# Attention loads in half as many transfers: q and k of four heads together, heads paired differently, and the division of two quads moved behind the next norms

## The chip, the cores and the metric

The kernel runs on one core of one Trainium2 chip. The metric is the device time of one execution in microseconds; lower is better. Times of "before" are the median of three runs, and one more execution was recorded by the hardware profiler. TensorE is called PE, VectorE DVE, ScalarE ACT, GpSimd POOL and SyncE SP.

## The reference

Attention with normalised queries and keys, followed by a feed-forward block on the heads joined together:

```python
batch, n_heads, seq, head_dim = (8, 12, 448, 64)
def rmsnorm(x, g):
    rms = np.sqrt(np.mean(x * x, axis=-1, keepdims=True) + 1e-06)
    return x / rms * g
q_n, k_n = (rmsnorm(q, g_q), rmsnorm(k, g_k))
scores = scale * np.matmul(q_n, k_n.transpose(0, 1, 3, 2))
scores = scores - np.max(scores, axis=-1, keepdims=True)
attn = np.exp(scores)
attn = attn / (np.sum(attn, axis=-1, keepdims=True) + 1e-09)
attn_out = np.matmul(attn, v)
x = np.ascontiguousarray(attn_out.transpose(0, 2, 1, 3)).reshape(B * S, H * D)
# x: 3584 x 768; h = x @ w_in (768 x 1024); SoLU; layer norm; @ w_out (1024 x 768)
```

q, k and v arrive in float32, the weights in float64.

## The kernel before

The work on the chip is `fast_path`, which has three stages that follow one another on PE: attention for 24 *quads* of four heads, the first feed-forward product and the second one (both by a scheme of seven products for eight). The change lies in the first stage, which ends at about 331 us.

A quad m consists of the pairs a = 2m and b = 2m + 1 of two heads each. For a pair n the steps are, with their lines in the profile:

- `load(n)` (L627): q and k of the two heads, each head in four quarters, go to 32 partitions at a time. That is eight transfers of 56 KB (L634) into a tile `qk`, of which five exist. `load_v(m)` (L639) brings v of a quad: one transfer for the first 384 keys (`v`, L647), two for the last 64 keys (`vl`, L651).
- `squares(n)` (ACT, L656), `row_sums(n)` (DVE, L664, tile `part`), and for a whole quad `fold_sums(m)` (POOL, L674 and L675, tile `ss`).
- `rsqrt_seed` (ACT, L694 and L695, tile `ny`), `rsqrt_step` (DVE, L701 to L704, tiles `nx` and `ny`), `normalise(n)` (POOL, L713, tile `qkn`), `qk_transpose(n)` (DVE, L723, tile `qkT`), `gain(n)` (ACT, L727).
- `scores(n, kc)` (PE, L812, tile `s`), three times for a pair, and `scores_last(m)` (PE, L825) for the last keys of both pairs. Behind each stands an exponential (ACT, L802, tile `E`).
- `add(n)` (DVE, L839, tile `es`), a part of the row sums.
- `values_last(m)` (PE, L854) and `values(n)` (PE, L865), E times v into the PSUM tile `o`. Two such tiles exist, one for each pair of a quad.
- `sums(m)` (PE, L884, tile `sm`), `inverse(m)` (DVE, L895 and L896, then copies on POOL, L903, tile `rc`), `divide(m)` (DVE, twice L910 and L911, reads both `o` and writes `xo`), `store_x(m)` (SP, L916) into the DRAM tensor `xd`, from which the second stage loads.

The first quad's q and k are loaded otherwise (`load_rows`, L732).

The order is written out by hand: within `tc.manual_schedule()` each engine carries out its instructions in the order in which the functions are called. In the body for quad m the norms of quad m + 1 are finished (`norms_next`), the squares and sums of quad m + 2 are taken, and q and k of quad m + 3 are loaded. `unit(f)` calls a piece of PE work; `later(1, f)` has f called after the next unit. So `later(1, lambda m=m: divide(m))` at the end of quad m puts the division behind scores(a, 0) of quad m + 1. For m > 4 `norms_next` comes before that, for m = 1, 2 and 3 after it (`early` is false).

All loads and stores of this stage are issued by SP, one after another, and an issue that has to wait holds up those behind it. Each transfer's landing is told by one of eight semaphores in turn, and an issue waits for the transfer that used its semaphore before.

Of the kernel before, what the change touches and what calls it, by code (L numbers as in the profile page):

```python
# [9 lines left out]
FP32 = mybir.dt.float32  # L10
# [3 lines left out]
AF = mybir.ActivationFunctionType  # L14
# [352 lines left out]
def fast_path(  # L367
# [38 lines left out]
    R = S // 4  # L406
# [12 lines left out]
    loads = first.enter_context(tc.tile_pool(name="loads", bufs=2))  # L419
# [8 lines left out]
    xd = [dram.tile([DM, S], FP32, name=f"xd{b}") for b in range(B)]  # L428
# [189 lines left out]
    st = {}  # L618
    quads = {}
    norms = {}  # L620

    def load(n):  # L627
        b, hp = divmod(n, NP)
        h0 = 2 * hp
        d = st[n] = {}  # L630
        d["qk"] = loads.tile([P, 2, NB, 32], FP32, tag="qk", name="qk", bufs=5)
        for s, src in enumerate((q, k)):
            for g in range(4):
                nc.sync.dma_start(  # L634
                    d["qk"][g * 32 : g * 32 + 32, s],
                    src[b, h0 + g // 2].rearrange("(b t) (x d) -> x t b d", t=32, x=2)[g % 2],
                )

    def load_v(m, queue=nc.sync):  # L639


        d = quads[m] = {}
        b, hp = divmod(2 * m, NP)
        src = v[b, 2 * hp : 2 * hp + 4]
        d["v"] = loads.tile([P, 4, NJ, D], FP32, tag="v", name="v", bufs=2)
        d["vl"] = loads.tile([P, 2, D], FP32, tag="vl", name="vl", bufs=2)
        queue.dma_start(  # L647
            d["v"].rearrange("p h j d -> p h (j d)"), src[:, 0 : NJ * P].rearrange("h (p j) d -> p h (j d)", j=NJ)
        )
        for i in range(2):  # L650
            nc.sync.dma_start(d["vl"][i * D : (i + 1) * D], src[2 * i : 2 * i + 2, NJ * P : S].rearrange("h p d -> p h d"))  # L651

    def squares(n):
        d = st[n]
        d["sq"] = work.tile([P, 2 * NB, 32], FP32, tag="sq", name="sq", bufs=2)
        nc.scalar.activation(d["sq"], d["qk"].rearrange("p s b d -> p (s b) d"), AF.Square)  # L656

# [48 lines left out]
    def normalise(n, e=nc.gpsimd):  # L706
        d = st[n]
        if ("one", n) in norms:
            y = norms["one", n]["y"]
        else:  # L710
            y = norms[n // 2]["y"][:, n % 2 * 2 * NB : (n % 2 + 1) * 2 * NB]
        d["qkn"] = work.tile([P, 2 * NB, 32], FP32, tag="qkn", name="qkn", bufs=2)
        e.tensor_tensor(  # L713
            d["qkn"],
            d["qk"].rearrange("p s b d -> p (s b) d"),
            y.rearrange("p b -> p b ()").to_broadcast([P, 2 * NB, 32]),
            OP.mult,
        )

# [12 lines left out]
    def load_rows(n, queues):  # L732
        b, hp = divmod(n, NP)
        d = st[n] = {}
        d["qk"] = xs.tile([P, 2, 4, P], FP32, tag="x", name="x")[0:R]
        for s, src in enumerate((q, k)):
            for h in range(2):
                queues[2 * s + h].dma_start(
                    d["qk"][:, s, :, h * D : (h + 1) * D], src[b, 2 * hp + h].rearrange("(j p) d -> p j d", p=R)
                )  # L740

    def square_rows(n, s, engine):
# [61 lines left out]
    def scores(n, kc):  # L804
        d = st[n]
        s = ps_t.tile([P, 2, 512], FP32, tag="t", name="s")

        for c in range(0, P, D):
            for h in range(2):
                hh = slice(h * D, (h + 1) * D)  # L810
                keys = slice(NJ * c + kc, NJ * (c + D - 1) + kc + 1, NJ)
                nc.tensor.matmul(  # L812
                    s[c : c + D, h, 0:S], d["qkT"][hh, 1, keys], d["qkT"][hh, 0, :],
                    start=True, stop=True,
                )
        exponentials(d, kc, s)
# [42 lines left out]
    def values(n):  # L859


        d = st[n]
        for kc in range(NJ):
            for h in range(2):
                nc.tensor.matmul(  # L865
                    d["o"][h * D : (h + 1) * D, :], quads[n // 2]["v"][:, n % 2 * 2 + h, kc], d["E", kc][:, h],
                    start=False, stop=(kc == NJ - 1),
                )

# [43 lines left out]

    def store_x(m):
        b, hp = divmod(2 * m, NP)
        nc.sync.dma_start(  # L916
            xd[b].rearrange("(c p) t -> p c t", p=P)[:, hp : hp + 2], quads.pop(m)["xo"]
        )

# [427 lines left out]
    setup()  # L1347
    load_gains()
    load_rows(1, (nc.sync, nc.sync, nc.scalar, nc.scalar))
    load(2)  # L1350
    load(3)
    load_v(0)
    load(4)
    load_norm_gain()
    load(5)
    with tc.manual_schedule():
        warm_up()
        square_rows(0, 0, nc.vector)
# [17 lines left out]
        for m in range(NQ):  # L1376
            a, b = 2 * m, 2 * m + 1
# [6 lines left out]
            next1 = m + 1 < NQ  # L1384
            next2 = m + 2 < NQ
            next3 = m + 3 < NQ
            if m == 0:
                unit(lambda: scores(a, 0))
                normalise_rows(1, 0)
                normalise_rows(1, 1)  # L1390
                unit(lambda: scores(a, 1))
                unit(lambda: scores(a, 2))
                for s in range(2):
                    transpose_rows(1, s)
                    take_rows(1, s)
# [12 lines left out]
                unit(lambda: scores(b, 1))  # L1408
                unit(lambda: scores(b, 2))
                rsqrt_seed(norms["one", 3])  # L1410
                rsqrt_step(norms["one", 3])
                normalise(3)
                qk_transpose(2)
                gain(2)
                add(b)
                load_v(1)
                load(6)
                load(7)
                unit(outputs)
# [12 lines left out]
            early = 3 < m and next1  # L1432
            def norms_next():
                rsqrt_seed(norms[m + 1])
                rsqrt_step(norms[m + 1])
                normalise(a + 2)
                normalise(b + 2)
# [4 lines left out]
                combine_in(x)  # L1442
            if next1:
                load_v(m + 1)
            unit(lambda: scores(a, 0))
            store_x(m - 1)
            if early:
                qk_transpose(a + 2)
                if next3:
                    load(a + 6)  # L1450
            if m == 3:
                norms_next()
            unit(lambda: scores(a, 1))
            if m == 2:
                norms_next()
            unit(lambda: scores(a, 2))
            if m == 3:
                qk_transpose(a + 2)
                load(a + 6)
            unit(lambda: scores_last(m))  # L1460
            if m == 3:
                norm_gain()
# [2 lines left out]
            unit(lambda: scores(b, 0))  # L1465
            if m == 1:
                norms_next()
                load(a + 6)
                load(b + 6)
            if m == 2:  # L1470
                qk_transpose(a + 2)
                load(a + 6)
            unit(lambda: scores(b, 1))
            if early or 1 < m < 4:
                qk_transpose(b + 2)
                if next3:
# [239 lines left out]
```

## Time and profile before

| | us |
|---|---|
| median of 3 runs | 823.92 (823.67 to 824.59) |
| the profiled execution | 824.07 |
| its span, from the first to the last instruction | 821.8 |
| PE busy in it | 800.8 |
| first `s` matmul of quad 1 / last matmul of the attention | 26.09 / about 331.6 |

The span is 2.3 us shorter than the execution's time. DMA packets of the execution: 272546, of which 190540 are under 512 bytes; q and k arrive in runs of 128 bytes.

```profile
qk<-in_q_dram SPq DMA_DIRECT2D x184, 56.0 KB, 2.6
qk<-in_k_dram SPq DMA_DIRECT2D x184, 56.0 KB, 2.4
v<-in_v_dram SPq DMA_DIRECT2D x24, 384.0 KB, 4.4
vl<-in_v_dram SPq DMA_DIRECT2D x48, 32.0 KB, 3.5
xd<-xo SPq DMA_DIRECT2D x24, 448.0 KB, 3.6
```

These lines of the list of transfers give the tile and its source, the queue, the number of transfers, the size of one, and the median time in us from issue to landing. A busy PE is read with care: its ends are modelled, and a gap shows only where an instruction really waited. In the timelines below a row joins neighbouring instructions of one line; its columns are start, length, engine, line, operation, tiles, shapes and count, and in brackets the idle time before it with what ended it.

### The profile page before, as it was taken

How to read it: one execution, taken by the hardware profiler on the slowest of the kernel's cores; microseconds unless marked ns; L12 is line 12 of the kernel's file. 1: busy time of each engine (PE TensorE's matmuls, PEld its weight loads, DVE VectorE, ACT ScalarE, POOL GpSimd, SP SyncE). 2: the span in 40 equal slices, each digit the busy share in tenths (PEclk: the TensorE clock that was granted, in tenths of full speed). 3: DMA queues.
4: the chain of work that ended last, by engine and by line, in shares of the span. 5: the costliest groups of instructions: out<-in, count | busy, mean ns of one | idle time of the engine just before them, and what ended most of it. 6: DMA issues, size and time to landing. Idle time of an engine off the chain costs nothing.

```text
span 821.8 us, 14997 instructions
## 1 busy us (share of the span) xinstructions
PE 800.8 (97%) x5030; PEld 469.7 (57%) x5030; DVE 616.3 (75%) x1217; ACT 475.3 (58%) x785; POOL 469.9 (57%) x635
## 2 busy tenths in 40 slices
PE   8989999999999999999999999999989999999996
PEld 4333444443344443444444444444689999999996
DVE  6867788887878888377878766677786866866945
ACT  6667778776867777366666644444514464464420
POOL 1334546555555647333356467777487777877861
PEclk9999999999999999999999999999999999999999
DMA  6678777877777664235665335453548466376312
GB/s 130 131 146 197 141 187 151 205 148 176 159 175 175 128 158 119 87 103 127 185 166 153 94 95 136 131 143 73 160 122 270 126 211 231 127 243 203 125 59 82
DMA packets 272546, 122.74 MB, mean 149 GB/s; under 512 B 190540, under 2 KB 257612, under 8 KB 272460
## 3 DMA queue, kind: packets, MB, share of 16 engines
q1 hardware_dynamic: 257276, 111.79, 52.9%
q10 hardware_dynamic: 15184, 9.90, 4.5%
q8 instruction: 42, 0.69, 0.4%
q14 instruction: 44, 0.36, 0.2%
HBM read 84.94 MB, written 36.70 MB: 148 GB/s over the span
## 4 chain that ended last, share of the span: by engine, by line
PE 71%; SPq 6%; DMA 5%; DVE 5%; issue 2%; POOL 2%; ACT 1%; DVEq 0%; POOLq 0%; ACTq 0%
PE A L1196 14%; PE A L982 11%; PE B L1196 7%; PE o L865 7%; PE s L812 7%; PE B L982 7%; SPq L634 5%; PE C L982 4%; PE D L982 4%; PE C L1196 4%; PE sm L884 3%; DMA v<-in_v_dram 2%; PE s L825 1%; PE o L854 1%; DMA qk<-in_k_dram 1%
## 5 line engine op out<-in xcount | busy, mean ns | idle before, releaser
L802 ACT ACTIVATE E<-s 128x896 f32<-128x896 f32 x168 | 139.0, 935 | 15.5 <-PE s L812 15.2
L812 PE MATMUL s<-qkT 64*64 64x448 f32 x1152 | 121.1, 547 | 1.5 <-ACT E L802 0.9
L865 PE MATMUL o<-E,v 128*64 128x448 f32 x576 | 113.5, 543 | 0.0
L674 POOL COPY ss<-part 32x56 f32<-32x56 f32 x88 | 42.1, 478 | 97.5 <-DVE part L664 94.8
L713 POOL TENSOR_TENSOR qkn<-qk,ny 128x896 f32<-128x896 f32 x46 | 77.1, 1697 | 27.5 <-DVE ny L704 12.0
L1071 POOL TENSOR_TENSOR he<-he,mhalf 128x1 f32<-128x1 f32 x28 | 27.6, 986 | 105.7 <-DVE he L1070 105.3
L1196 PE MATMUL B<-w_out,sums 128*128 128x192 f32 x392 | 80.4, 328 | 3.3 <-DVE P L1258 2.1
L812 PEld LDWEIGHTS s<-qkT 64*64 64x64 f32 x1152 | 47.7, 163 | 60.7 <-ACT E L802 30.9
L1196 PE MATMUL A<-w_out,sums 128*128 128x192 f32 x392 | 80.6, 329 | 1.0 <-POOL sums L1177 0.7
L865 PEld LDWEIGHTS o<-E,v 128*64 128x64 f32 x576 | 39.2, 137 | 72.7 <-issue 65.2
L982 PE MATMUL B<-w_in,xsum 128*128 128x512 f32 x168 | 76.7, 593 | 0.7 <-POOL he L1071 0.7
L982 PE MATMUL A<-w_in,xg 128*128 128x512 f32 x168 | 74.7, 593 | 0.1
L1196 PEld LDWEIGHTS B<-w_out,sums 128*128 128x128 f32 x392 | 66.9, 191 | 3.9 <-DVE P L1258 2.4
L1053 ACT ACTIVATE u<-h,hmax 128x1024 f32<-128x1024 f32 x28 | 32.2, 1148 | 63.3 <-DVE hmax L1047 63.2
L1196 PEld LDWEIGHTS A<-w_out,sums 128*128 128x128 f32 x392 | 66.8, 191 | 1.7 <-POOL sums L1177 1.6
L982 PEld LDWEIGHTS B<-w_in,xsum 128*128 128x128 f32 x168 | 31.8, 190 | 41.2 <-issue 38.3
L664 DVE TENSOR_REDUCE part<-sq 128x28 f32<-128x896 f32 x46 | 48.6, 1079 | 8.5 <-ACT sq L656 6.5
L982 PEld LDWEIGHTS A<-w_in,xg 128*128 128x128 f32 x168 | 31.8, 190 | 40.5 <-issue 39.1
L723 DVE STREAM_TRANSPOSE qkT<-qkn 128x896 f32<-128x896 f32 x46 | 48.9, 1092 | 6.6 <-POOL qkn L713 6.6
L839 DVE TENSOR_TENSOR es<-E 128x896 f32<-128x896 f32 x48 | 53.3, 1113 | 0.5 <-ACT E L802 0.5
L656 ACT ACTIVATE sq<-qk 128x896 f32<-128x896 f32 x46 | 43.5, 987 | 7.6 <-DMA qk<-in_k_dram 7.3
L563 POOL TENSOR_TENSOR w_out<-w_out 128x384 f32<-128x384 f32 x44 | 45.3, 1036 | 1.3
(151 smaller groups left out, 1625.3 us busy)
## 6 DMA issues: line engine op xcount, KB each, us to landing
ur<-ud SPq DMA_DIRECT2D x60, 256.0 KB, 4.6
ud<-ub SPq DMA_DIRECT2D x112, 128.0 KB, 2.3
xd<-xo SPq DMA_DIRECT2D x24, 448.0 KB, 3.6
qk<-in_q_dram SPq DMA_DIRECT2D x184, 56.0 KB, 2.6
qk<-in_k_dram SPq DMA_DIRECT2D x184, 56.0 KB, 2.4
v<-in_v_dram SPq DMA_DIRECT2D x24, 384.0 KB, 4.4
out_dram<-P SPq DMA_DIRECT2D x19, 384.0 KB, 3.9
raw<-in_moe_w_in_dram SPq DMA_DIRECT2D x12, 512.0 KB, 5.4
```

Of the source, the lines that this page charges most:

```text
L563: nc.gpsimd.tensor_tensor(o, p, q, OP.subtract)
L656: nc.scalar.activation(d["sq"], d["qk"].rearrange("p s b d -> p (s b) d"), AF.Square)
L664: nc.vector.tensor_reduce(norms[m]["part"][:, i], st[n]["sq"], AX, OP.add)
L674: e.tensor_copy(ss[g * 32 : g * 32 + 32], part[o * 32 : o * 32 + 32])
L713: e.tensor_tensor(d["qkn"], d["qk"].rearrange("p s b d -> p (s b) d"), y.rearrange("p b -> p b ()").to_broadcast([P, 2 * NB, 32]), OP.mult,)
L723: nc.vector.transpose(d["qkT"].rearrange("p s t -> p (s t)"), d["qkn"].rearrange("p b d -> p (b d)"))
L802: nc.scalar.activation(d["E", kc], s[:, :, 0:S], AF.Exp)
L812: nc.tensor.matmul(s[c : c + D, h, 0:S], d["qkT"][hh, 1, keys], d["qkT"][hh, 0, :], start=True, stop=True,)
L839: nc.vector.tensor_tensor(d["es"], d["E", 0], d["E", 1], OP.add)
L865: nc.tensor.matmul(d["o"][h * D : (h + 1) * D, :], quads[n // 2]["v"][:, n % 2 * 2 + h, kc], d["E", kc][:, h], start=False, stop=(kc == NJ ...
L982: nc.tensor.matmul(k[bank], a[:, c], w_in[i][:, c], start=begin and c == 0, stop=c == HD - 1, skip_group_check=not begin,)
L1196: nc.tensor.matmul(k[bank], a[:, c].rearrange("p a i -> p (a i)"), w_out[:, area, i, c], start=begin and c == 0, stop=c == KC - 1, skip_gr ...
```

## The change

Four edits, all in the first stage:

1. `load(m)` loads a quad. Its tile holds both pairs, and a transfer carries one quarter of two heads (28 blocks of 32 numbers for a partition instead of 14): eight transfers of 112 KB for a quad instead of sixteen of 56 KB. Four tiles exist. For the two heads to lie at an even distance in DRAM, pair i of quad m consists of the heads 4m + i and 4m + i + 2 (before: 4m + 2i and 4m + 2i + 1). The indices of `v`, of `load_rows` and of the rows of `xd` follow, and `store_x` needs two transfers of 64 partitions.
2. `load_v(m)` fetches the last keys for the quads m and m + 1 together, in every other quad.
3. The loads of the quads 1, 2 and 3 and of v for the quads 0 and 1 stand ahead of everything, that of quad 4 at the start of quad 1; later ones go on being issued three quads ahead, once a quad.
4. The divisions of quads 1 and 2 no longer follow scores(a, 0) of the next quad. They follow `norms_next` there, with the store behind them.

```diff
-    def load(n):
-        b, hp = divmod(n, NP)
-        h0 = 2 * hp
-        d = st[n] = {}
-        d["qk"] = loads.tile([P, 2, NB, 32], FP32, tag="qk", name="qk", bufs=5)
+    def heads(x, m, n=4):
+        return x.rearrange("b h s d -> (b h) s d")[4 * m : 4 * m + n]
+
+    def load(m):
+        qk = loads.tile([P, 2, 2, NB * 32], FP32, tag="qk", name="qk", bufs=4)
         for s, src in enumerate((q, k)):
+            rows = heads(src, m).rearrange("(h i) (b t) (x d) -> h x t (i b) d", h=2, t=32, x=2)
             for g in range(4):
                 nc.sync.dma_start(
-                    d["qk"][g * 32 : g * 32 + 32, s],
-                    src[b, h0 + g // 2].rearrange("(b t) (x d) -> x t b d", t=32, x=2)[g % 2],
+                    qk[g * 32 : g * 32 + 32, s].rearrange("p i (b d) -> p (i b) d", d=32), rows[g // 2, g % 2]
                 )
+        for i in range(2):
+            st[2 * m + i] = {"qk": qk[:, :, i]}
...
     def load_v(m, queue=nc.sync):
         d = quads[m] = {}
...
-        d["vl"] = loads.tile([P, 2, D], FP32, tag="vl", name="vl", bufs=2)
...
-        for i in range(2):
-            nc.sync.dma_start(d["vl"][i * D : (i + 1) * D], src[2 * i : 2 * i + 2, NJ * P : S].rearrange("h p d -> p h d"))
+        if m % 2 == 0:
+            vl = loads.tile([P, 4, D], FP32, tag="vl", name="vl", bufs=2)
+            two = heads(v, m, 8)[:, NJ * P : S].rearrange("(h i) p d -> i p h d", i=2)
+            for i in range(2):
+                nc.sync.dma_start(vl[i * D : (i + 1) * D], two[i])
+                lasts[m + i] = vl[:, 2 * i : 2 * i + 2]
+        d["vl"] = lasts.pop(m)
 
     def squares(n):
...
-        nc.scalar.activation(d["sq"], d["qk"].rearrange("p s b d -> p (s b) d"), AF.Square)
+        nc.scalar.activation(d["sq"].rearrange("p (s b) d -> p s (b d)", s=2), d["qk"], AF.Square)
...
         e.tensor_tensor(
-            d["qkn"],
-            d["qk"].rearrange("p s b d -> p (s b) d"),
-            y.rearrange("p b -> p b ()").to_broadcast([P, 2 * NB, 32]),
+            d["qkn"].rearrange("p (s b) d -> p s b d", s=2),
+            d["qk"].rearrange("p s (b d) -> p s b d", d=32),
+            y.rearrange("p (s b) -> p s b ()", s=2).to_broadcast([P, 2, NB, 32]),
             OP.mult,
         )
...
-                    d["o"][h * D : (h + 1) * D, :], quads[n // 2]["v"][:, n % 2 * 2 + h, kc], d["E", kc][:, h],
+                    d["o"][h * D : (h + 1) * D, :], quads[n // 2]["v"][:, n % 2 + 2 * h, kc], d["E", kc][:, h],
...
     def store_x(m):
         b, hp = divmod(2 * m, NP)
-        nc.sync.dma_start(
-            xd[b].rearrange("(c p) t -> p c t", p=P)[:, hp : hp + 2], quads.pop(m)["xo"]
-        )
+        xo = quads.pop(m)["xo"]
+        rows = xd[b].rearrange("(g h i d) t -> h d g i t", h=2, i=2, d=D)
+        for h in range(2):
+            nc.sync.dma_start(rows[h][:, hp // 2], xo[h * D : (h + 1) * D])
...
     load_rows(1, (nc.sync, nc.sync, nc.scalar, nc.scalar))
+    load(1)
+    load_v(0)
     load(2)
+    load_norm_gain()
+    load_v(1)
     load(3)
-    load_v(0)
-    load(4)
-    load_norm_gain()
-    load(5)
     with tc.manual_schedule():
...
                 add(b)
-                load_v(1)
-                load(6)
-                load(7)
                 unit(outputs)
...
             if next1:
                 load_v(m + 1)
+            if m == 1:
+                load(m + 3)
             unit(lambda: scores(a, 0))
-            store_x(m - 1)
+            if m not in (2, 3):
+                store_x(m - 1)
             if early:
                 qk_transpose(a + 2)
                 if next3:
-                    load(a + 6)
+                    load(m + 3)
             if m == 3:
                 norms_next()
+                divide(m - 1)
+                store_x(m - 1)
             unit(lambda: scores(a, 1))
             if m == 2:
                 norms_next()
+                divide(m - 1)
+                store_x(m - 1)
             unit(lambda: scores(a, 2))
             if m == 3:
                 qk_transpose(a + 2)
-                load(a + 6)
+                load(m + 3)
...
             if m == 1:
                 norms_next()
-                load(a + 6)
-                load(b + 6)
             if m == 2:
                 qk_transpose(a + 2)
-                load(a + 6)
+                load(m + 3)
             unit(lambda: scores(b, 1))
             if early or 1 < m < 4:
                 qk_transpose(b + 2)
-                if next3:
-                    load(b + 6)
...
             inverse(m)
-            if next1:
+            if next1 and m not in (1, 2):
                 later(1, lambda m=m: divide(m))
```

More of the change, by code (lines that the diff above doesn't have):

```diff
@@ L620, in fast_path @@
     norms = {}
-    def load(n):
-        b, hp = divmod(n, NP)
-        h0 = 2 * hp
-        d = st[n] = {}
-        d["qk"] = loads.tile([P, 2, NB, 32], FP32, tag="qk", name="qk", bufs=5)
+    lasts = {}
+    def heads(x, m, n=4):
+        return x.rearrange("b h s d -> (b h) s d")[4 * m : 4 * m + n]
+    def load(m):
+        qk = loads.tile([P, 2, 2, NB * 32], FP32, tag="qk", name="qk", bufs=4)
         for s, src in enumerate((q, k)):
+            rows = heads(src, m).rearrange("(h i) (b t) (x d) -> h x t (i b) d", h=2, t=32, x=2)
             for g in range(4):
                 nc.sync.dma_start(
-                    d["qk"][g * 32 : g * 32 + 32, s],
-                    src[b, h0 + g // 2].rearrange("(b t) (x d) -> x t b d", t=32, x=2)[g % 2],
-                )
+                    qk[g * 32 : g * 32 + 32, s].rearrange("p i (b d) -> p (i b) d", d=32), rows[g // 2, g % 2]
+                )
+        for i in range(2):
+            st[2 * m + i] = {"qk": qk[:, :, i]}
     def load_v(m, queue=nc.sync):
         d = quads[m] = {}
-        b, hp = divmod(2 * m, NP)
-        src = v[b, 2 * hp : 2 * hp + 4]
         d["v"] = loads.tile([P, 4, NJ, D], FP32, tag="v", name="v", bufs=2)
-        d["vl"] = loads.tile([P, 2, D], FP32, tag="vl", name="vl", bufs=2)
         queue.dma_start(
-            d["v"].rearrange("p h j d -> p h (j d)"), src[:, 0 : NJ * P].rearrange("h (p j) d -> p h (j d)", j=NJ)
-        )
-        for i in range(2):
-            nc.sync.dma_start(d["vl"][i * D : (i + 1) * D], src[2 * i : 2 * i + 2, NJ * P : S].rearrange("h p d -> p h d"))
+            d["v"].rearrange("p h j d -> p h (j d)"),
+            heads(v, m)[:, 0 : NJ * P].rearrange("h (p j) d -> p h (j d)", j=NJ),
+        )
+        if m % 2 == 0:
[5 more added lines that the diff above has]
+        d["vl"] = lasts.pop(m)
     def squares(n):
@@ L738, in load_rows @@
                 queues[2 * s + h].dma_start(
-                    d["qk"][:, s, :, h * D : (h + 1) * D], src[b, 2 * hp + h].rearrange("(j p) d -> p j d", p=R)
+                    d["qk"][:, s, :, h * D : (h + 1) * D], src[b, 4 * (hp // 2) + hp % 2 + 2 * h].rearrange("(j p) d -> p j d", p=R)
                 )
```

## The prediction

> **What bounds the kernel now.** I began with the page. Its first lines say that TensorE is hardly ever idle, so a change to loads can only win back the gaps that TensorE still has.
>
> ```profile
> PE 800.8 (97%) x5030; PEld 469.7 (57%) x5030; DVE 616.3 (75%) x1217; ACT 475.3 (58%) x785; POOL 469.9 (57%) x635
> ```
>
> Next I read the timeline of PE alone and noted where each quad m begins, which is the first `s` matmul of scores(2m, 0): m = 1 to 5 at 26.09, 40.66, 55.70, 70.38 and 84.65 us, m = 13, 14, 15 at 188.00, 202.99 and 216.84. Between m = 5 and m = 13 lie 8 quads in 103.35 us, 12.92 each; the chain of waits shows 12.90 for one of them (97.62 to 110.52), with no gap on PE. So 12.90 is what a quad costs in PE work, and the rest is lost: m = 1 14.57 (1.67 lost), m = 2 15.04 (2.14), m = 3 14.68 (1.78), m = 4 14.27 (1.37), m = 13 14.99 (2.09), m = 14 13.85 (0.95). That is 10.0 us, the most that a change to the attention's loads and order can bring after quad 0. The gaps, from the same timeline:
>
> ```profile
> 29.85 0.98 PE L825 MATMUL s<-qkT 64*64 64x448 f32 x8 [1.24 <-ACT E L802]
> ...
> 55.19 0.59 PE L884 MATMUL sm<-es,ones 128*32 128x224 f32 x8 [1.23 <-DVE es L839]
> ...
> 73.84 0.98 PE L825 MATMUL s<-qkT 64*64 64x448 f32 x8 [0.95 <-ACT E L802]
> ...
> 202.47 0.59 PE L884 MATMUL sm<-es,ones 128*32 128x224 f32 x8 [1.89 <-DVE es L839]
> ```
>
> Each gap was then followed back on the engine that it names. The timeline of ACT gives two causes in the loads (start, length, and in brackets the idle time before it):
>
> ```profile
> 28.04 0.95 ACT L656 ACTIVATE sq<-qk 128x896 f32<-128x896 f32 x1 [0.80 <-DMA qk<-in_k_dram]
> ...
> 199.35 0.95 ACT L656 ACTIVATE sq<-qk 128x896 f32<-128x896 f32 x1 [3.65 <-DMA qk<-in_k_dram]
> ```
>
> ACT works in order, so behind the first stand the exponentials of quad 1, and behind the second, by way of `part` and `es` on DVE, the sums of quad 13. Why are the loads late? SP's own timeline shows a queue without a hole; one quad's worth:
>
> ```profile
> 87.53 0.43 SPq L647 DMA_DIRECT2D v<-in_v_dram  x1
> 88.00 1.25 SPq L651 DMA_DIRECT2D vl<-in_v_dram  x2
> 89.34 0.54 SPq L916 DMA_DIRECT2D xd<-xo  x1
> 90.00 3.06 SPq L634 DMA_DIRECT2D qk<-in_q_dram  x4
> 93.10 2.64 SPq L634 DMA_DIRECT2D qk<-in_k_dram  x4
> 95.85 1.99 SPq L634 DMA_DIRECT2D qk<-in_q_dram  x4
> 97.88 2.04 SPq L634 DMA_DIRECT2D qk<-in_k_dram  x4
> ```
>
> From 87.53 to 99.92 are 12.4 us of issuing in a quad of 12.90, before a w_in load (0.48) is added in some quads. SP falls behind until a load is late, which is the stall at 199. Meanwhile the table of stretches puts the 16 DMA engines at 0.70 busy from 85 to 98. SP, not the engines, is full.
>
> The other cause, in m = 2 and 3, is the order on DVE and POOL:
>
> ```profile
> 43.97 0.65 DVE L910 STREAM_TRANSPOSE r<-rc 128x448 f32<-128x448 f32 x1 [1.82 <-POOL rc L903]
> ...
> 46.53 0.18 DVE L701 TENSOR_SCALAR nx<-ss 128x56 f32<-128x56 f32 x1
> ...
> 49.40 1.11 DVE L723 STREAM_TRANSPOSE qkT<-qkn 128x896 f32<-128x896 f32 x1 [1.86 <-POOL qkn L713]
> ```
>
> DVE first waits for `rc` and divides the last quad (43.97 to 46.61), then does the Newton step, though `ny` was ready at 43.97; `qkn` on POOL, both `qkT`, `es` and the sums on PE follow, all late.
>
> **What the Trainium skill says.** "DMA: Bandwidth & Descriptors", Rules for kernel authors, advises to coalesce many small transfers into a large one. The same page, section Issuing engines are not separate DMA queues, holds that the time on the sequencer to start a DMA "is usually small relative to the DMA itself". The trace differs: a transfer of `qk` keeps SP 0.477 us (median, view of line L634), and by the bound below the engines at most 0.57. Its section on why a DMA increments its semaphore by 16 says that the number of engines follows from the slowest dimension of both sides and that one descriptor is one contiguous run. Here the slowest dimension stays 32 for `qk`, becomes 64 for the stores, and runs stay 128 bytes, so the same engines get the same pieces, twice as many per transfer. No run here shows the new shape.
>
> **The change part by part.** (1) *Issues.* Per quad 16 `qk` issues become 8, two `vl` issues become two per two quads, one store becomes two. Removed: 8 of 0.52 (0.477 and a gap of 0.04) = 4.2, and 0.63 of `vl`; added: 0.54. SP goes from 12.4 to about 8.1 us of 12.90. Whether an issue grows with its number of descriptors, the trace tells only indirectly: `v` (512 runs) takes 0.39 to 0.43, `vl` (128 runs) 0.60, ACT's `xg` (768 runs) about 0.4. I take no growth; the bound on the other side is a doubling to 1.0, which would give back all 4.2.
>
> (2) *The engines.* 0.70 of 13 us is 9.1 us per quad for everything, so a small transfer costs at most 9.1/16 = 0.57 and a big one 1.14. Per quad that stays 9.1 of 12.90: no more bytes, no fewer. SP also waits, before each issue, for the transfer eight places earlier (the built program's list of waits); eight big ones in flight are a quad's loads, so the queue then runs at the engines' pace, not below it.
>
> (3) *Start.* The first 8 `qk` transfers now carry pairs 2 and 3, and squares(2) needs all. Issued from 3.94; with 9.1 us of engine time they are in by 13.0. squares(2) began at 14.60 without a wait: 1.6 us spare, and beyond it each us costs one. load(2) follows by 22.1 (squares(4) at 24.43) and load(3) by 31.2 (squares(6) at 35.03). `v` for quad 0, due at 17.3, goes out right after the first eight.
>
> (4) *m = 1.* squares(5) starts when gain(3) ends, 27.25 for 28.04: 0.8 gained, passed on by the exponentials to the scores (29.85), by divide(0) to the vl matmuls. Quad 2 begins at 39.86.
>
> (5) *m = 2.* With all 0.8 earlier, `ny` is ready at 43.2; the three operations that need it end at 43.95, POOL makes `qkn` to 45.65 and 47.35 (1.70 each) instead of 51.05. The moved divide (2.64) now runs 43.95 to 46.6. This adds a wait: PE's vl matmuls write the `o` banks that divide(1) reads, and would be due at 45.75; the second waits until 46.65, and with it all of PE. So 0.9 is paid there, values begin at 47.4 (47.57 before), sums at 52.06. DVE then does `qkT` to 48.7, `es` to 49.7, `part`, and the second `es` to 51.7; PE needs it at 53.6, so the gap of 1.23 goes. Sums end at 54.09: quad 2 lasts 14.23, 0.81 less.
>
> (6) *m = 3.* The lead is 1.61. `ny` comes after the first exponential, at 56.7; step to 57.45, divide to 60.15, `qkn` to 59.2 and 60.85, `qkT` to 62.3, `es` 63.3 and 65.35, `part` to 66.4. The vl matmuls come at 60.76, after the divide; sums at 66.27 wait for nothing and end at 68.3. Quad 3 lasts 14.21, 0.47 less.
>
> (7) *m = 4.* `part` ended at 70.80 and let ACT wait 3.98 us for `ss`, which made the gap of 0.95. Now `ss` is there at 67.9, before the first scores, and the quad runs like a steady one, 12.95: 1.32 less. Together (4) to (7): 3.4 us.
>
> (8) *m = 13 and 14.* The loads go out three quads ahead and SP has 4.8 us per quad to spare, so nothing is late: 2.09 + 0.95 = 3.04 gained.
>
> (9) *Cost taken as nothing.* `qkn` and `sq` get patterns of one more level. A POOL copy of 32x14 takes 0.19, so two pieces instead of one cost at most 0.2 per `qkn`; the divide covers the first, and 0 to 0.1 per quad remains in m = 2 and 3; it could also be free. The stores of m = 2 and 3 wait for the later divide, with load(5) and load(6) behind them on SP: issued from 46.7 and 60.2, in by 56 and 70 at 1.14 each, used at 62 and 75. If that cover went, ACT would wait there instead. The PE, ACT and POOL orders are otherwise unchanged, and later stages are only shifted.
>
> The sum is 3.4 + 3.04 = 6.4 us off the profiled execution of 824.07 (span 821.8 and 2.3 around it): 817.6. The median of the runs, 823.92, lies 0.15 below, so 817.5.
>
> **Rivals.** *A, issue grows with size.* If a big issue takes 1.0, SP stays at 12 us per quad. The order of DVE still helps, and m = 1 starts late as now: 0.81 + 0.47 + 1.32 = 2.6, and perhaps half of 3.04 since the loads stand a little further ahead: 4.1, giving 819.8. For it: I have no 896-run transfer. Against: 0.4 us for 768 runs. *B, the divide is in the way.* If the vl matmuls wait as long in m = 3 too, and POOL's longer `qkn` takes the rest, only 0.8 + 3.04 stay, so 820.1. Against: in m = 3 the divide ends 0.6 before PE needs the banks. *C, the other side: the transfers become the bound.* Place: SP's queue in every steady quad, where an issue waits for the landing eight earlier. If big transfers follow one another every t us, a quad's loads take 8t + 2.1 + 0.3 of gaps, which passes 12.90 at t = 1.31; from t = 1.35 on, 20 quads lose more than (5) to (7) gain and 1.7 besides. At t = 1.40 it is 20 x 0.7 - 2.6 = 11.4 slower, 835. For it: more runs in flight may serve worse, unseen here. Against: the bound of 1.14 from a quad where every other transfer was counted as free. *D*: the lateness has another cause and nothing moves, 823.9.
>
> **How the numbers follow.** Mine 0.72, A 0.12, B 0.05, C 0.08, D 0.03. My own case spans 815.3 (half of what is still lost in m = 1 to 3 goes too) to 819.5 (the start's margin or POOL costs 2); up to 821.0 the range takes in A and B, and leaves out C, D and some tails, about 0.17. A measurement of this kernel tells no change from 0.2%, 1.65 us. Faster: mine, nearly all of A, and B, 0.87; the same: D and a rest, 0.05; slower: C, 0.08.
>
> **What would show it.** Right: no idle time of ACT's `sq` for `qk`; 12.9 us per quad from m = 4 to 23; SP with holes of 4 us per quad; `qk` issues still near 0.5; PE waiting once for `xo` in m = 2; the gap at `sm` in m = 2 gone. Wrong: SP full or issues of 1 us (A); PE waiting for `xo` in m = 3 (B); landings of `qk` more than 8 us after issue and `sq` waiting in steady quads (C); squares(2) waiting before 15 us, which would eat into (3).

## The result, and the profile after

The changed kernel takes 816.50 us (median of 4, 815.47 to 818.07) against 823.79 us (median of 4, 823.41 to 824.59): a ratio of 0.9912, with a 95% interval of 0.9894 to 0.9930. It is 7.3 us faster; 817.5 was forecast. The profiled execution took 815.47 us with a span of 813.7.

The page's line of the engines has PE busy for 797.9 us of a span that is 8.1 us shorter, 98% of it; the other engines do the same work as before:

```profile
PE 797.9 (98%) x5030; PEld 468.4 (58%) x5030; DVE 617.0 (76%) x1217; ACT 473.9 (58%) x785; POOL 469.0 (58%) x635
```

The starts of the quads, read from the timeline of PE as before, give their lengths (us):

| quad | before | after | forecast |
|---|---|---|---|
| 1 | 14.57 | 13.66 | 13.77 |
| 2 | 15.04 | 14.26 | 14.23 |
| 3 | 14.68 | 14.12 | 14.21 |
| 4 | 14.27 | 12.90 | 12.95 |
| 5 to 12, each | 12.92 | 12.90 | 12.90 |
| 13 | 14.99 | 12.90 | 12.90 |
| 14 | 13.85 | 12.89 | 12.90 |
| 23 (last) | 12.14 | 12.95 | as before |
| end of the attention | at 331.51 | at 325.46 | |

So 6.05 us of the 8.1 are won in the attention. The other 2 lie behind it, where the two programs do the same: 1.4 between the end of the attention and the last instruction of an engine (484.7 us before, 483.3 after), and 0.7 between that instruction and the end of the span (5.6 and 4.9). Before, PE's granted clock has a mean of 0.91 in the stretch from 600 to 620 us, and after it is 1.00 there. The runs below show that this dip comes and goes with the execution, and costs about 1 us.

SP's timeline of one quad (start and length of each group of issues in us):

```profile
94.49 0.39 SPq L647 DMA_DIRECT2D v<-in_v_dram  x1
98.55 1.24 SPq L925 DMA_DIRECT2D xd<-xo  x2
99.89 3.05 SPq L636 DMA_DIRECT2D qk<-in_q_dram  x4
102.98 2.57 SPq L636 DMA_DIRECT2D qk<-in_k_dram  x4
105.59 0.73 SPq L510 DMA_DIRECT2D raw<-in_moe_w_in_dram  x1
106.42 0.38 SPq L647 DMA_DIRECT2D v<-in_v_dram  x1
106.85 1.30 SPq L655 DMA_DIRECT2D vl<-in_v_dram  x2
```

Between 94.88 and 98.55 SP stands still: it has nothing left to issue but a store whose data is not ready. The view of waits, restricted to SP and to 60 to 300 us, says so in one line (total, times, longest):

```profile
SPq L925 <- DVE xo L917: 72.3, 19, 5.1
```

That is 3.8 us of room in each quad. In the kernel before, that list has no wait for `xo` at all; its longest entry is

```profile
SPq L634 <- DMA v<-in_v_dram: 1.8, 8, 0.4
```

There, over the attention, `sq` waited for `qk` five times, 7.3 us in all; in the changed kernel no `sq` waits for `qk`.

PE's timeline in quads 2 and 3 shows the wait that was forecast and one gap that stays:

```profile
45.55 1.83 PE L860 MATMUL o<-E,vl 64*64 64x448 f32 x8
...
58.18 2.57 PE L818 MATMUL s<-qkT 64*64 64x448 f32 x24 [0.58 <-ACT E L808]
```

The eight `vl` matmuls of quad 2 take 1.83 us for 0.93: the second half waits for the division of quad 1. And the last quad has a gap that was not there before:

```profile
315.41 0.98 PE L831 MATMUL s<-qkT 64*64 64x448 f32 x8 [0.39 <-ACT E L808]
```

ACT's timeline tells where it comes from. After:

```profile
312.65 0.84 ACT L950 ACTIVATE xsum<-xg 128x768 f32<-128x768 f32 x1 [4.44 <-DMA xg<-xd]
```

Before:

```profile
317.64 0.84 ACT L943 ACTIVATE xsum<-xg 128x768 f32<-128x768 f32 x1 [2.57 <-DMA xg<-xd]
```

Counted from the start of quad 22, `xg` landed after 10.5 us in the kernel before and after 12.4 us in the changed one, and ACT, which works in order, has the exponentials of quad 23 behind `xsum`.

### The profile page after: what moved, and what is told of

The parts are those of the page before. It is cut to its first block, busy times and chain, and to the rows that moved or that the text cites. A ratio compares the mean times of both kernels' runs of the same rounds, so it can differ in the third digit from the quotient of the medians.

```text
span 813.7 us, 14586 instructions
## 1 busy us (share of the span) xinstructions
PE 797.9 (98%) x5030; PEld 468.4 (58%) x5030; DVE 617.0 (76%) x1217; ACT 473.9 (58%) x785; POOL 469.0 (58%) x635
## 4 chain that ended last, share of the span: by engine, by line
PE 88%; DVE 5%; POOL 2%; DMA 2%; ACT 2%; issue 1%; SPq 0%; DVEq 0%; POOLq 0%; ACTq 0%
PE A L1203 14%; PE A L989 13%; PE o L871 13%; PE s L818 12%; PE B L989 8%; PE B L1203 7%; PE sm L890 5%; PE C L989 4%; PE D L989 4%; PE C L1203 3%; PE o L860 2%; PE s L831 2%; DMA xg<-xd 1%; ACT E L808 1%; DVE bs L1072 1%
## 5 line engine op out<-in xcount | busy, mean ns | idle before, releaser
L719 POOL TENSOR_TENSOR qkn<-qk,ny 128x896 f32<-128x896 f32 x46 | 77.1, 1697 | 21.2 <-DMA qk<-in_k_dram 12.0
L871 PEld LDWEIGHTS o<-E,v 128*64 128x64 f32 x576 | 39.2, 137 | 72.7 <-issue 67.3
L1203 PE MATMUL A<-w_out,s 128*128 128x192 f32 x224 | 45.5, 326 | 0.0
```

What stands on the lines that cost most here:

```text
L719: e.tensor_tensor(d["qkn"].rearrange("p (s b) d -> p s b d", s=2), d["qk"].rearrange("p s (b d) -> p s b d", d=32), y.rearrange("p (s b) - ...
L871: nc.tensor.matmul(d["o"][h * D : (h + 1) * D, :], quads[n // 2]["v"][:, n % 2 + 2 * h, kc], d["E", kc][:, h], start=False, stop=(kc == NJ ...
L1203: nc.tensor.matmul(k[bank], a[:, c].rearrange("p a i -> p (a i)"), w_out[:, area, i, c], start=begin and c == 0, stop=c == KC - 1, skip_gr ...
```

## The experiments

Each run lists the median and, with its 95% interval, the ratio to the kernel before, which ran beside it on the same chip; the ratio is not the quotient of two medians. Two traces are compared by their quads.

### One part alone

The first two take the change apart. The order alone, on the kernel before:

```
+            if m not in (2, 3):
                 store_x(m - 1)
...
             if m == 3:
                 norms_next()
+                divide(m - 1)
+                store_x(m - 1)
...
-            if next1:
+            if next1 and m not in (1, 2):
                 later(1, lambda m=m: divide(m))
```

> The kernel before with one part of the change: quads 1 and 2 are divided (and stored) right after norms_next of quads 2 and 3, all loads as before. Theory (two separate causes, order on DVE and issues on SP): the gap at sm in quad 2 and the gap at the last s of quad 4 go, some 0.8 + 0.5 + 1.4 = 2.6 us gained, the late load in quad 1 (about 0.9) stays, and the late load at quads 13 and 14 (3.0) stays or comes a little earlier, since SP is as full as before: about 821.2. Rival (everything comes from SP): about 823.8, no gain. Rival (everything comes from the order): about 816.5.

Measured: 823.02 us, ratio 0.9998 (0.9986 to 1.0011). Nothing. Yet quads 2 to 4 are as short as in the changed kernel (14.33, 14.12, 12.89), and quad 5 begins at 81.00 instead of 84.65. What follows is in ACT's timeline:

```profile
169.19 0.95 ACT L656 ACTIVATE sq<-qk 128x896 f32<-128x896 f32 x1 [1.55 <-DMA qk<-in_k_dram]
...
183.92 0.95 ACT L656 ACTIVATE sq<-qk 128x896 f32<-128x896 f32 x1 [2.42 <-DMA qk<-in_k_dram]
...
198.75 0.95 ACT L656 ACTIVATE sq<-qk 128x896 f32<-128x896 f32 x1 [3.35 <-DMA qk<-in_k_dram]
...
226.64 0.95 ACT L656 ACTIVATE sq<-qk 128x896 f32<-128x896 f32 x1 [2.71 <-DMA qk<-in_k_dram]
```

Ten squares wait for `qk` in all, 16.2 us, against five and 7.3 us before, and the quads from 5 to 16 give back all of the lead: 13.34, 13.85, then 14.73, 14.83, 13.85, 14.04 and 13.85 for quads 12 to 16. The attention ends at 333.00. SP issues for 12.4 us per quad and a `w_in` load on top, so what the quads gain on it early they wait for later.

The loads alone are the changed kernel with the divisions at their ordinary place:

```
-            if m not in (2, 3):
-                store_x(m - 1)
+            store_x(m - 1)
...
-            if next1 and m not in (1, 2):
+            if next1:
```

> The changed kernel with the other part alone: the new transfers and the new order of loads, the divisions of quads 1 and 2 at their ordinary place. Theory: 0.9 in quad 1 and 3.0 at quads 13 and 14 are gained, the gaps of quads 2 to 4 stay, and 0.8 is lost in the last quad: some 3.1 us less than before, about 820.5; together with the gain of the divisions alone it should give the whole. Rival (the loads' relief is all there is): 816.5.

Measured: 819.41 us, ratio 0.9953 (0.9940 to 0.9967), 3.9 us less than before. Quads 2 to 4 stay long (15.04, 15.03, 14.27; quad 3 is even 0.35 longer than in the kernel before), with the same gaps in PE's timeline:

```profile
54.21 0.58 PE L890 MATMUL sm<-es,ones 128*32 128x224 f32 x8 [1.23 <-DVE es L845]
...
73.21 0.98 PE L831 MATMUL s<-qkT 64*64 64x448 f32 x8 [0.95 <-ACT E L808]
```

Then every quad up to 21 takes 12.90. So the parts do not add: 0 and 3.9 make 7.3 together. The order's gain is real, 2.65 us in quads 2 to 4 of the run with the order alone and 3.4 (7.3 less 3.9) on top of the loads, but only SP's room lets it be kept. The expectation for the order alone (821.2) missed this.

### How much room SP needs

Each q or k transfer in two halves, with the tiles, buffers, order and pairing of the change:

```
-                nc.sync.dma_start(
-                    qk[g * 32 : g * 32 + 32, s].rearrange("p i (b d) -> p (i b) d", d=32), rows[g // 2, g % 2]
-                )
+            for i in range(2):
+                for g in range(4):
+                    nc.sync.dma_start(
+                        qk[g * 32 : g * 32 + 32, s, i].rearrange("p (b d) -> p b d", d=32), rows[g // 2, g % 2, i]
+                    )
```

> The changed kernel with each q or k transfer issued as two halves of one pair of heads each (16 issues of qk per quad as before, with the same bytes, tiles, buffers, pairing and order). Theory (the number of issues on SP is the cause): an issue takes about 0.5 us again, SP goes from some 8.7 to 12.9 us per quad of 12.9 and has no hole, falls behind, and squares wait for qk again in some quads: 1 to 4 us lost, 817.5 to 820.5. Rival (the four tiles, the earlier start and the new order are the cause, not the count): 816.5.

Measured: 829.69 us, ratio 1.0085 (1.0066 to 1.0104): slower than the kernel before, and far more than expected. Two causes are in the trace. One is a single stall in quad 2, which lasts 21.94 us. DVE's timeline:

```profile
50.48 0.62 DVE L918 TENSOR_TENSOR xo<-o,r 128x448 f32<-128x448 f32 x1 [6.16 <-DMA xd<-xo]
```

and SP's:

```profile
37.74 4.44 SPq L637 DMA_DIRECT2D qk<-in_q_dram  x8
42.24 4.37 SPq L637 DMA_DIRECT2D qk<-in_k_dram  x8
46.71 1.26 SPq L926 DMA_DIRECT2D xd<-xo  x2
```

`xo` has one buffer. The store of quad 0 stands behind the 16 issues of load(4), and the division of quad 1 cannot overwrite `xo` before it has landed. The other is what was looked for: squares wait for `qk` 19 times, 18.6 us, and from quad 11 to 20 all quads but one take 13.2 to 14.1.

To part the two, load(4) goes behind the store:

```
-            if m == 1:
-                load(m + 3)
             unit(lambda: scores(a, 0))
             if m not in (2, 3):
                 store_x(m - 1)
+            if m == 1:
+                load(m + 3)
```

> The kernel with the halves again (16 issues of qk per quad), and load(4) of quad 1 placed behind scores(2, 0) and the store of quad 0 instead of ahead of them. In the run with the halves quad 2 took 21.94 us, because the store of quad 0 stood on SP behind 16 issues and the division of quad 1 waited for it (6.16 us on xo). Theory (that wait is one cause, the full SP from quad 11 on another): quad 2 takes about 14.3 again, 7.7 us less, and the late loads from quad 11 on stay, somewhat larger as SP is met sooner: 822 to 824, that is about 6 to 7 us over the changed kernel for the number of issues alone. Rival (all of the halves' loss is that one wait): about 816.5 to 817.

Measured: 828.32 us (824.27 to 831.13), ratio 1.0063 (1.0040 to 1.0085). Quad 2 takes 14.26 again, but half of what that saved comes back: quads 8 to 21 lose 11.8 us between them, and the attention ends at 337.44 (341.28 with the stall, 325.46 in the changed kernel). The whole is some 12 us over the changed kernel, more than the 6 to 7 expected, and it looks like the run with the order alone: what is gained ahead of a full SP is lost behind it. The rival, that the stall was all, is out. This kernel issues as many transfers per quad as the kernel before and still ends 5 us behind it; its groups of 16 `qk` issues take 10.8 to 11.6 us (from 173 to 199 us) where they took 9.7 in the quad shown of before, and why some issues are longer there stays open. It is not that the DMA engines are full: between 60 and 290 us their mean share is 0.75 in this run and 0.82 in the changed kernel, which loses nothing.

Half of the way: q goes in four transfers of two heads, only k in halves, with the store first.

```
+            if s == 0:
+                ...
+                    nc.sync.dma_start(
+                        qk[g * 32 : g * 32 + 32, s].rearrange("p i (b d) -> p (i b) d", d=32), both[g // 2, g % 2]
+                    )
+                continue
```

> The kernel with the halves and the store first, but with q in four transfers of two heads each again and only k in halves: 12 issues of qk per quad instead of 16 or 8. SP's need per quad is then 4 of 0.56 and 8 of 0.48 and the gaps, some 2 us less than with 16. Theory (SP is a threshold: it costs nothing as long as a quad's issues fit into 12.90 us): 816 to 817, as with 8 issues, and no squares that wait for qk. Rival (each issue costs its share, through the DMA engines or the waits between transfers): half way between 8 and 16 issues, about 822.

Measured: 817.89 us, ratio 0.9938 (0.9916 to 0.9961). The quads are those of the changed kernel to 0.04 us, 12.90 from 4 to 21, no square waits, and the attention ends at 325.42. SP's waits from 60 to 300 us:

```profile
SPq L933 <- DVE xo L925: 44.7, 19, 3.8
```

That is 2.4 us of room per quad with 12 issues, 3.8 with 8, and none with 16. For the attention the number of issues is a threshold, not a price per issue. The whole time is nevertheless some 1.8 us above that of the changed kernel beside it (816.05, below), outside the 816 to 817 expected. In the one trace none of that is in the loads: the last instruction on an engine ends at 808.73, and at 808.75 in the first trace of the changed kernel, but the span ends 7.3 us after it instead of 4.9. What fills the 2.4 us the trace does not tell, and that the other executions share it is not shown.

Whether the fourth tile matters, the room to load further ahead, one number tells: `bufs=4` becomes `bufs=3` for `qk`.

> The changed kernel with three tiles for q and k of a quad instead of four, all else as it is. Theory (the relief is the number of issues on SP): a load has to wait for the tile of a quad that is already normalised, so nothing changes, 816.5 and quads of 12.90. Rival (it is the fourth tile, the room to load further ahead, that removes the late loads): squares wait for qk in some quads and 1 us or more is lost, 817.5 or more.

Measured: 815.86 us, ratio 0.9928 (0.9902 to 0.9954). The quads up to 22 are the same and no square waits, so the fourth tile is not what removes the late loads. The last quad takes 13.28 for 12.95; whether that comes from the tiles is not shown.

### Room made another way

The kernel with the order alone, its small transfers and old pairing, and v with its last keys issued by ACT:

```
-                load_v(m + 1)
+                load_v(m + 1, nc.scalar)
...
-            nc.sync.dma_start(d["vl"][i * D
+            queue.dma_start(d["vl"][i * D
```

> The kernel before with the divisions of quads 1 and 2 moved, all of its 16 small transfers of q and k with the old pairing, and the three transfers of v and its last keys per quad issued by ACT instead of SP. Theory (room on SP is what counts, whichever way it is made): SP needs 12.9 - 1.8 = 11.1 us per quad, no load is late after quad 4, the quads take 12.90, and the time is near that of the changed kernel, 816 to 818 (ACT pays 3 issues per quad of some 0.1 to 0.5 us, at the quad's begin where it waits 1.2 us for the first scores). Rival (the new transfers are better served by the DMA engines, or the pairing matters): as with the divisions alone, about 823. Rival (the issues on ACT delay the exponentials): 0.5 us per quad lost, 827 or more.

Measured: 876.14 us, ratio 1.0661 (1.0632 to 1.0689). The theory failed, and the rival that ACT's issues delay the exponentials holds in part. They take 1.65 us per quad (0.38 for v, 1.27 for two of its last keys), and from 60 to 345 us the exponentials stood behind them nine times, 14.1 us in all. The larger waits are of SP, over the same stretch:

```profile
SPq L634 <- DMA v<-in_v_dram: 64.2, 16, 6.1
```

By the program's waits, an issue waits for the transfer eight places earlier, whichever engine issues that. ACT issues v only when it gets there, behind the exponentials of the quad before, and SP, which was to run ahead, is tied to it; in that stretch squares wait 39.2 us for `qk`. So this run says nothing about room on SP, and room made in another way than by fewer issues stays untested. It says that in this program, where the transfers of all queues take the eight semaphores in turn, moving some of the loads to a busier queue ties the whole stream to it.

### A second trace of each

> The kernel before once more, for a second trace of it. If its late loads come from SP being as full as a quad is long, then where they fall is a matter of chance: squares wait for qk again, but not in the same quads or as long as in the first trace. If they come from the order of the program, the same quads (1, 13, 14) are long, by the same amounts (14.57, 14.99 and 13.85 us).

Measured: 825.56 us, a single execution. Squares wait again, six times, in part at other places (ACT's timeline, all but one of 1.06 us at 38.38):

```profile
182.93 0.95 ACT L656 ACTIVATE sq<-qk 128x896 f32<-128x896 f32 x1 [1.15 <-DMA qk<-in_k_dram]
197.53 0.95 ACT L656 ACTIVATE sq<-qk 128x896 f32<-128x896 f32 x1 [2.86 <-DMA qk<-in_k_dram]
...
224.25 0.95 ACT L656 ACTIVATE sq<-qk 128x896 f32<-128x896 f32 x1 [1.53 <-DMA qk<-in_k_dram]
...
250.70 0.95 ACT L656 ACTIVATE sq<-qk 128x896 f32<-128x896 f32 x1 [1.26 <-DMA qk<-in_k_dram]
...
277.55 0.95 ACT L656 ACTIVATE sq<-qk 128x896 f32<-128x896 f32 x1 [1.67 <-DMA qk<-in_k_dram]
```

Quad 1 lasts 13.66, as in the changed kernel: its late load of the first trace does not come back. The waits at 182.93 and 197.53, in quads 12 and 13, do: they were 1.45 and 3.65 us in the first trace. Quads 13 and 14 are long again (14.19, 13.85), and now also 16, 18 and 20 (13.82, 13.56, 13.86): 4.9 us lost from quad 13 on, not 3.04. So neither expectation holds as it stands: where SP first falls behind comes again, what follows does not. The attention ends at 332.36. Quads 2 to 4 are the same to 0.02 us (15.06, 14.69, 14.29): these come from the order of the program, the others from SP.

> The changed kernel once more, beside the others on one chip, for a second trace and more times: 816.5 expected, the same quad lengths as in its first trace (13.66, 14.26, 14.12 us for quads 1 to 3, 12.95 for the last, 12.90 between), since nothing in it should stand at an edge.

Measured: 816.05 us, ratio 0.9912 (0.9885 to 0.9939). Quads 1 to 3 take 13.66, 14.27 and 14.13, the last 12.88, all between 12.90 (12.27 for quad 22, as ever), the attention ends at 325.47 (325.46). The kernel with room repeats itself; the kernel before does not. Their times say the same: beside one another on this chip, the kernel before spreads from 819.22 to 825.55 us in 13 runs, the changed one from 815.31 to 817.00 in 6.

### The last quad, and a faster version

`load_x(0)` reads what quads 0 to 2 stored long ago, and stands behind the store of quad 21. It is put ahead of it:

```
+            if m == NQ - 2:
+                load_x(0)
             if m not in (2, 3):
                 store_x(m - 1)
...
             if m == NQ - 2:
-                load_x(0)
                 sizes(0)
```

> The changed kernel with load_x(0) issued in quad 22 ahead of the store of quad 21 instead of behind it and the loads. Theory (the 0.8 us of the last quad is lost because x of the first token group stands on SP behind a store that now is two issues and waits for the division): ACT's sizes(0) no longer waits 4.4 us, E of quad 23 comes in time, the last quad lasts about 12.1 instead of 12.95, and the time falls by about 0.8, to 815.7. Rival (the last quad is late for another reason, such as the clock or PE itself): 816.5, no change.

Measured: 815.68 us, ratio 0.9906 (0.9890 to 0.9922). The last quad lasts 12.14, as it did before the change, and the attention ends at 324.73. The 0.8 us are found; against the changed kernel's own times, 816.50 and 816.05, which were not taken beside this run, the difference of the whole is at the edge of what can be told.

Then the wait of PE in quad 2. `rc` of quad 1 stands on POOL behind the copies for `ss`; the row sums of the last pair are put behind the inverse, and the division of quad 1 goes back to its ordinary place (the edit stands on that of the run before):

```
-            if m not in (2, 3):
+            if m != 3:
                 store_x(m - 1)
...
             if m == 2:
                 norms_next()
-                divide(m - 1)
-                store_x(m - 1)
...
-            if next2:
+            if next2 and m != 1:
                 row_sums(b + 4)
                 fold_sums(m + 2)
...
             inverse(m)
-            if next1 and m not in (1, 2):
+            if m == 1:
+                row_sums(b + 4)
+                fold_sums(m + 2)
+            if next1 and m != 2:
                 later(1, lambda m=m: divide(m))
```

> The changed kernel with x of the first token group ahead of the store (as in the run before, 815.7), and in quad 1 the row sums of the last pair and their folding placed behind the inverse of quad 1, with its division at its ordinary place ahead of the Newton step of quad 2. Theory (the 0.9 us that PE waits in quad 2 for the division of quad 1 comes from rc standing on POOL behind ss): rc is ready about 0.9 us earlier, the division ends at 44.2 instead of 46.4, PE does not wait at the vl matmuls, qkn is 0.9 later but es still comes in time for the sums: quad 2 lasts 13.3 instead of 14.27, about 814.8 in all. Rival (the later qkn and es take the place of the wait): 815.7 or a little more, with a gap at sm in quad 2.

Measured: 815.47 us, ratio 0.9928 (0.9902 to 0.9953). The division ended at 44.4 and the `vl` matmuls took 0.93, but PE's timeline has a new gap:

```profile
44.74 1.82 PE L818 MATMUL s<-qkT 64*64 64x448 f32 x16 [0.89 <-ACT E L808]
```

On ACT, `ny` was next in order and waited for `ss`, now later, with the third exponential behind it. Quad 2 lasts 14.10: a wait changed its name. So `norms_next` goes one block of scores later in quads 2 and 3:

```
+            unit(lambda: scores(a, 1))
             if m == 3:
                 norms_next()
                 divide(m - 1)
                 store_x(m - 1)
-            unit(lambda: scores(a, 1))
+            unit(lambda: scores(a, 2))
             if m == 2:
                 norms_next()
-            unit(lambda: scores(a, 2))
```

> The kernel with the inverse first (815.5), where PE waited 0.89 us in quad 2 for an exponential, because ny stood on ACT ahead of it and waited for ss. Here norms_next goes one block of scores later in quads 2 and 3. Theory (the exponential is only behind ny in ACT's order): the gap of 0.89 in quad 2 falls to some 0.15 and that of 0.58 in quad 3 goes too, the division still ends before the vl matmuls and es before the sums: 1.0 to 1.3 us less, about 814.3. Rival (qkn or es is late next): no gain, with a gap at sm or at vl in quads 2 or 3, 815.5.

Measured: 814.99 us (814.17 to 815.23), ratio 0.9897 (0.9870 to 0.9923), beside 816.05 (815.31 to 817.00) for the changed kernel beside it. It is the fastest of all. Quad 2 lasts 13.65, 0.6 less than in the changed kernel. In quad 3 the gap stays,

```profile
57.62 2.57 PE L818 MATMUL s<-qkT 64*64 64x448 f32 x24 [0.75 <-ACT E L808]
```

since `ny` only moved from the second exponential to the third; that half of the expectation failed, and the quad takes 14.27 for 14.13.

## Why the prediction was right

The mechanism, room on SP and the order on DVE, was right, and the sum of 6.4 us stands against 6.05 at the end of the attention in the first pair of traces and 6.89 in the second. That the whole came within 1 us of the forecast is in part luck: the last quad lost 0.8 us that were not foreseen, and some 2 us came off behind the attention, where nothing was forecast. By its steps:

(1) *Issues.* No growth was assumed. There is some: a transfer of `qk` keeps SP 0.557 us (median) with 896 runs, 0.477 with 448. With two stores and occasional longer issues, SP needs some 9.1 us per quad (12.90 less 3.8 of waiting), not 8.1. It cost nothing, because 12 issues fit too. Rival A needed a doubling. One issue alone is a fifth of the 2.4 us from issue to landing; it is the sum of them over a quad that was full.

(2) *The engines.* A transfer of 112 KB lands 3.0 to 3.1 us after its issue, one of 56 KB 2.4 to 2.6. The assumption that the engines' time per quad stays as it was failed: between 60 and 290 us their share is 0.82 for 0.76, at 170 GB/s for 167, which makes 10.6 us of 12.90 for 9.8 (the 0.70 of the prediction was a stretch below this mean). The pieces themselves are the same: the packets under 512 bytes fell by 2944, just 16 for each of the 184 transfers fewer. The margin to rival C was thinner than thought, but no square waited and C did not show. The page on "DMA: Bandwidth & Descriptors" of the Trainium skill, which advises in its Rules for kernel authors to coalesce small transfers, is borne out here. What counted in these runs was the time of the issuing queue, for the engines were not relieved.

(3) *Start.* squares(2) began at 14.58 without a wait, as forecast.

(4) *Quad 1.* 0.91 us were won for 0.8, but the cause was only half right. The late load at 28.04 of the first trace is not in the second, nor with the order alone: the new loads take away a risk there, not a fixed cost.

(5) to (7) *Quads 2 to 4.* 14.26, 14.12 and 12.90 for 14.23, 14.21 and 12.95. The wait of 0.9 at the `vl` matmuls came as worked out, the gap at `sm` went. (In the program `norms_next` stands ahead of the division from quad 4 on, not only for m > 4, so there was nothing to move there.) What the sum hid: these gains were counted as if they held by themselves (rival A too counted 2.6 for the order with SP full). The order alone brought nothing in the end. The total was right since both parts are in the change.

(8) *Quads 13 and 14.* 3.05 for 3.04 by the first trace; the second would have said 4.9 from quad 13 on. The cause was right, the size was one draw. That the loads were issued late, and did not land slowly, the first trace of the kernel before shows at quad 13:

```profile
194.82 2.04 SPq L634 DMA_DIRECT2D qk<-in_k_dram  x4
```

ACT was ready for the square at 195.70, when two of these four were still to be issued; the last was issued at 196.38, and the square began 3.0 us after that.

(9) *Later stages are only shifted.* This failed: the last quad lost 0.81 us. The step looked at SP's queue for the stores of quads 2 and 3, but not at what stands behind the store of quad 21. The store there waits for the division, it is two issues now, and `xg`, counted from the start of quad 22, is issued 0.9 us later and lands 1.9 later; why its way from issue to landing takes 1.0 more is open. POOL's `qkn` at 1697 ns was unchanged, as assumed.

The medians differ by 7.3; in the first pair of traces the attention gives 6.05 of it. The rest lies behind the attention. About 1 us of it is the clock: both traces of the kernel before show the dip between 600 and 620 us, both of the changed kernel do not. In the run with three tiles, which has it, the time from the attention's end to the last instruction was 484.3 us, 483.3 in the changed kernel. The dip does not belong to the old loads: the order alone, with the old loads, lacks it, and four runs with the new pairing have it (the loads alone, x first, three tiles, the halves with the store first). It begins within 1.3 us after the end of two waits of PE, 1.16 and 2.15 us, between the second and the third stage, which stand in every trace with the dip or without. Another 0.7 is the time behind the last instruction: 5.6 to 5.8 us in the three traces with the old loads on SP, 4.9 to 5.0 in those with the new pairing, but for the 7.3 with k in halves. Its cause is open, and so is that of the 0.4 us that remain.

## What to carry to other kernels

Add up one period of each issuing queue, as for an engine. A queue whose issues fill the period is easily overlooked, since its issues count as nobody's busy time; here it took back, as late loads at places that in part changed, all that the order had gained. Test a change of order together with room on the queue, for alone it can measure nothing. Once there is room, more of it need bring nothing: 2.4 and 3.8 us gave the same quads. When a store is split or moved, list all that stands behind it on its queue, to the end of the loop and beyond.

## What the runs showed of the hardware that was not expected

A transfer with twice the 128-byte runs (896 for 448) took 17% more of SP's time to issue, 0.557 us for 0.477 (medians), not twice. The same bytes in half as many transfers did not relieve the DMA engines: their share rose from 0.76 to 0.82. Loads issued by ACT cost it 0.4 to 0.6 us each, and in this program tied SP's own issues to their landing (64.2 us of waits). A program that differs only in its transfers and the place of one load can end 2.4 us later behind its last instruction (7.3 for 4.9 us in the trace with k in halves), of which no engine shows anything.
